# Inverse transform of a spectral-filter and feed-forward kernel: first step split over two sums of 64 frequencies, last step over 16 classes, both as pairs of 64-row matmuls

## The chip, the cores and the metric

The kernel runs on one core of a Trainium2 chip. The metric is device time in microseconds of one execution, taken as the median over runs. One profiled execution of the kernel before was recorded too; all durations of single instructions come from it.

TensorE (PE) multiplies; VectorE (DVE) and ScalarE (ACT) do elementwise work and empty the matmul results out of PSUM; GpSimd (POOL) and SyncE (SP) mainly issue DMAs here. Each engine works through its own instruction list in the order in which the program wrote it.

## The reference

The input x has 2048 rows (s) and 1024 columns (d). It is normalised by row to xn. One branch is a two-dimensional real Fourier filter, the other a feed-forward layer; the result is x + filter * silu(feed-forward).

```python
xn = _layernorm(x, axis=-1)
X = rfft2(xn, axes=(-2, -1)) * (w_r + 1j * w_i)      # w: 2048 x 513
s = irfft2(X, (2048, 1024), axes=(-2, -1))
h = silu(einsum("bsd,df->bsf", xn, w1))              # w1: 1024 x 3584
g = silu(einsum("bsf,fd->bsd", h, w2))               # w2: 3584 x 1024
return x + s * g
```

## The kernel before

Numbers are kept as two fp16 halves, so that each product of fp32 quality is three matmuls (high by high, high by low, low by high). Two stages of feed-forward matmuls form the backbone of TensorE's list. The first (`mm1`, L420, tile `pa`) makes the hidden layer in 112 groups of 24 matmuls of 512 columns. The second (`mm2`, L498 to L500, tile `pb`) runs seven products of a Strassen-like scheme, each in eight blocks; a block is two halves of 21 matmuls of 512 columns, and the 56 blocks make 112 halves.

The Fourier work is woven between these matmuls. Transforms are cut into a matmul over part of the index and a small butterfly on VectorE. In order: the forward transform over d (`fd_gen`, tiles `fa`, `V`, `R`), the forward transform over s with the product by the filter (`f_gen`, 16 tiles `u`: matmuls `fx` at L902 to L904, the complex product at L972 to L986, first inverse radix-4 butterflies into `Z`, and `zq`, the two fp16 halves of the result, which goes to DRAM as `zd`), a small correction for the edge frequencies (`edge_gen`), and the inverse (`i_gen`, four chunks `c`).

A chunk of the inverse loads `zt` (2 MB of `zd`) and its matrix `kk`. It has two parts. In the first, `mat(g)` (L1110 to L1118, tile `iu`) makes 24 matmuls of 256 columns, each a sum over 128 frequencies of s; `post(g)` (L1120 to L1130) copies half of the PSUM tile with ScalarE, forms sums and differences on VectorE and a radix-4 butterfly; `split(g)` (L1132 to L1137) makes the two fp16 halves `us`. In the second, `mat2(p)` (L1141 to L1147, tile `id`) makes 24 matmuls of 256 columns over d, in 8 classes of frequencies with 128 rows, and `bfly(p)` (L1149 on) combines the classes and hands the finished 128 rows to the output. Each of `mat` and `mat2` fills a PSUM tile of two banks; there are two such tiles (`pt`), so a `mat` waits until the one two before it has been emptied.

The order of all this is written out by a planner while the program is built. `meter` (L179) adds the planned cost of each instruction to a clock for TensorE and one for VectorE, by `COST` (L177): a fixed part and a part for each element. `work()` (L1274) is called after each of the 112 groups of `mm1` and after each half of a block of `mm2`. It lets the weight loaders move, and then takes up to three steps from the background list `bg`, which holds the Fourier generators in order. A step is what a generator does up to its next `yield`; a `yield PAUSE` ends the call:

```python
clock["dve"] = max(clock["dve"], clock["pe"] - 1.0)
for _ in range(3):
    if clock["dve"] > clock["pe"] + LEAD or hold[0] or slot(bg) == PAUSE:
        break
```

with `LEAD` 1.0. A tile of `f_gen` is four steps. A chunk of `i_gen` is six steps for `mat`, `post` and `split`, a load of the next chunk, a PAUSE, and five steps for `mat2` and `bfly`; each chunk but the first begins with four PAUSEs. Between `f_gen` and the first chunk stand the steps of the edge and eight PAUSEs, in which `zt` is loaded. The 128 rows that `bfly` finishes are stored to DRAM (`sd`) and read back (`fs`) when the product that completes the same rows of the other branch is through: products 4 and 5 for chunks 1 and 3, product 6 for chunk 0 in its first four blocks and for chunk 2, the last of the order, in its last four. What is left on `bg` when the 56 blocks are through is written out behind them (L1417).

Queues: SP issues the loads of weights, of `vq`, `wq`, `zt`, `kk`, `cis`, and the output; POOL issues the stores `hd`, `zd` and some weight loads; the loads of `ht` and `kq` are issued from ScalarE's list, in order with its activations.

Of the kernel before, what the change touches and what calls it, by code (L numbers as in the profile page):

```python
# [43 lines left out]
def make_constants():  # L44
# [17 lines left out]
    kc = np.stack(_halves(k, 2.0**14), 3)

    ci = np.zeros((128, 4, 2, 256))
    idx = np.arange(64)[:, None]
    dd = np.arange(128)[None, :]
    alt = np.where(dd[0] % 2 == 0, 1.0, -1.0)
    for g in range(4):
        for h, cl in enumerate((0, 4) if g == 0 else (g, 8 - g)):
            kd = 8 * idx + cl  # L70
            ph = 2 * np.pi * ((kd * dd) % 1024) / 1024
            co, si = 2 * np.cos(ph), 2 * np.sin(ph)
            r = slice(64 * h, 64 * h + 64)
            sg = 1 if h == 0 else -1
            if g == 0:
                ci[r, g, 0] = np.concatenate([co, sg * co], 1)
                ci[r, g, 1] = np.concatenate([-si, -sg * si], 1)
            else:
                ci[r, g, 0] = np.concatenate([co, sg * si], 1)
                ci[r, g, 1] = np.concatenate([-si, sg * co], 1)  # L80
# [16 lines left out]
def spectral_ffn(ctx, tc, x, w_r, w_i, w1, w2, ca, kc, ci, tw, pm, out):  # L97
    nc = tc.nc
# [773 lines left out]
    def f_gen():  # L872
        bp = B["p"]

        def load_k(q):
# [48 lines left out]

        def high_z(u):
            q, j = u // 4, u % 4
            if j == 0:
# [1 line left out]
            nc.scalar.activation(zqs[q][:, 0, :, 16 * j:16 * j + 16], zs_[u], AF.Copy, scale=zs)
# [522 lines left out]
```

## Time and profile before

| | us |
|---|---|
| runs, median (lowest to highest) | 1291.36 (1288.75 to 1295.92) |
| profiled execution, span from first to last instruction | 1291.9 |
| TensorE busy in the span | 1264.8 (98%) |
| VectorE busy | 958.6 (74%) |
| ScalarE busy | 463.9 (36%) |
| GpSimd busy | 242.3 (19%) |
| DMA moved | 298.84 MB, mean 231 GB/s |
| TensorE busy with `iu` and `id`, 384 matmuls each | 45.3 and 43.2 |

The profile gives no time of its execution other than the span. Busy time is a union: matmuls overlap, so a group's busy time is less than count times mean. The `mm1` stage lies from about 23 to 645 us, the `mm2` stage from 645 us to the end, `f_gen` from about 585 to 885 us and the inverse from 945 to 1202 us.

### The profile page before, as it was taken

What the parts mean: (1) busy time and instruction counts of PE and PEld (TensorE: products, weight loads), DVE (VectorE), ACT (ScalarE), POOL (GpSimd) and SP (SyncE); (2) the same over time, 40 slices, a digit from 0 to 9 for tenths busy, and PEclk for the clock granted to TensorE, in tenths of its full rate; (3) what the DMA queues carried; (4) which work ended last, traced back from release to release, by engine and by line L of the source; (5) the groups of instructions that cost most, each with busy time, mean ns of one, the idle gap of its engine ahead of it and who ended that gap; (6) DMA issues with size and microseconds to landing.
All of it is one profiled execution on the core that took longest, in us unless ns stands there. A gap on an engine that the chain in (4) does not pass through costs nothing.

```text
span 1291.9 us, 18825 instructions
## 1 busy us (share of the span) xinstructions
PE 1264.8 (98%) x6991; PEld 656.7 (51%) x6991; DVE 958.6 (74%) x1964; ACT 463.9 (36%) x572; POOL 242.3 (19%) x389
## 2 busy tenths in 40 slices
PE   8999999999999999999999999999979999999997
PEld 5544445444544454445455555554445555656444
DVE  6688898899879898867679798993165565867544
ACT  4864343343545565534242311220131321333111
POOL 1231222223233443241221010104110100000000
PEclk9998999999999999999999999999989999999999
DMA  7576476555766896579889999984996799675995
GB/s 232 132 188 178 123 227 191 164 149 181 230 194 236 278 296 205 190 230 269 179 252 259 270 278 199 336 213 146 305 259 229 218 323 339 241 285 167 313 360 187
DMA packets 174955, 298.84 MB, mean 231 GB/s; under 512 B 38928, under 2 KB 91920, under 8 KB 174224
## 3 DMA queue, kind: packets, MB, share of 16 engines
q1 hardware_dynamic: 132464, 163.34, 42.5%
q0 software_dynamic: 26560, 82.86, 21.3%
q10 hardware_dynamic: 15840, 51.45, 11.3%
q8 instruction: 55, 0.90, 0.3%
q14 instruction: 36, 0.29, 0.1%
HBM read 189.06 MB, written 104.33 MB: 227 GB/s over the span
## 4 chain that ended last, share of the span: by engine, by line
PE 82%; DMA 8%; DVE 5%; ACT 2%; issue 2%; POOL 1%; SPq 0%; ACTq 0%; DVEq 0%; POOLq 0%
PE pa L420 39%; PE pb L498 10%; PE pb L499 10%; PE pb L500 10%; PE iu L1117 3%; PE id L1146 3%; DMA jr<-ws 2%; DMA hd_one<-hoone 2%; PE fx L902 1%; DMA zt<-zd 1%; ACT xp L657 1%; DMA jr<-in_B_w_dram 1%; DVE w L219 1%; DMA ht<-hd_sum 1%; PE fx L904 1%
## 5 line engine op out<-in xcount | busy, mean ns | idle before, releaser
L420 PE MATMUL pa<-xnT,w 128*128 128x512 f16 x2688 | 587.7, 380 | 5.6 <-DMA xnT<-xs 3.2
L420 PEld LDWEIGHTS <-w 128*128 128x128 f16 x2688 | 263.2, 98 | 319.0 <-issue 8.3
L498 PE MATMUL pb<-w,ht 128*128 128x512 f16 (+1 forms) x798 | 299.5, 375 | 0.2 <-DMA ht<-hd_sum_d 0.2
L499 PE MATMUL pb<-w,ht 128*128 128x512 f16 (+1 forms) x798 | 299.5, 375 | 0.0
L500 PE MATMUL pb<-w,ht 128*128 128x512 f16 (+1 forms) x798 | 299.5, 375 | 0.0
L429 ACT ACTIVATE h<-pa,s 128x512 f32<-128x512 f32 x112 | 75.8, 680 | 142.5 <-PE pa L420 135.7
L500 PEld LDWEIGHTS <-ht 128*128 128x128 f16 x798 | 78.1, 98 | 91.1
L498 PEld LDWEIGHTS <-ht 128*128 128x128 f16 x798 | 78.2, 98 | 88.5 <-DMA ht<-hd_sum_d 0.7
L499 PEld LDWEIGHTS <-ht 128*128 128x128 f16 x798 | 78.1, 98 | 87.8
L216 ACT ACTIVATE w<-jr,sc 128x512 f16<-128x512 f32 x98 | 67.7, 713 | 85.3 <-DMA jr<-in_B_w_dram 39.8
L219 DVE SCALAR_TENSOR_TENSOR w<-jr,sc,w 128x512 f16<-128x512 f32 x98 | 72.1, 748 | 25.9 <-ACT w L216 25.8
L219 DVE SCALAR_TENSOR_TENSOR hoone<-h,hs,hoone 128x2048 f16<-128x2048 f32 x28 | 65.8, 2348 | 19.6 <-ACT hoone L216 19.6
L452 POOL DMA_DIRECT2D hd_sum<-hosum x52 | 38.0, 767 | 209.8 <-DVE hosum L219 101.7
L216 ACT ACTIVATE hoone<-h,hs 128x2048 f16<-128x2048 f32 x28 | 55.9, 1997 | 40.3 <-DMA hd_one<-hoone 27.9
L216 ACT ACTIVATE hosum<-hr,hs 128x1536 f16<-128x1536 f32 x28 | 44.1, 1574 | 59.4 <-DVE hr L459 32.1
L452 POOL DMA_DIRECT2D hd_one<-hoone x52 | 45.5, 875 | 86.5 <-DVE hoone L219 52.5
L380 POOL DMA_DIRECT2D jr<-in_B_w_dram x28 | 24.6, 966 | 165.0 <-DMA jr<-in_B_w_dram 129.6
L458 DVE TENSOR_TENSOR hr<-h 128x1024 f32<-128x1024 f32 x28 | 34.2, 1223 | 28.0 <-ACT h L429 27.8
L1117 PE MATMUL iu<-kk,zt 128*128 128x256 f16 x384 | 45.3, 280 | 8.7 <-issue 8.7
L219 DVE SCALAR_TENSOR_TENSOR hosum<-hr,hs,hosum 128x1536 f16<-128x1536 f32 x28 | 50.8, 1814 | 1.9 <-ACT hosum L216 1.9
L216 ACT ACTIVATE w<-w1r,rs 128x1024 f16<-128x1024 f32 x28 | 32.0, 1146 | 49.6 <-DVE rs L247 20.2
L579 ACT ACTIVATE pl<-pl,c 128x512 f32<-128x512 f32 (+1 forms) x26 | 16.9, 682 | 89.5 <-DVE pl L558 45.9
(195 smaller groups left out, 1686.0 us busy)
## 6 DMA issues: line engine op xcount, KB each, us to landing
w1r<-in_B_w_dram SPq DMA_DIRECT2D x28, 512.0 KB, 6.2
w2m<-in_B_w_dram SPq DMA_DIRECT2D x28, 512.0 KB, 5.0
ht<-hd_dif ACTq DMA_DIRECT2D x32, 448.0 KB, 7.9
jr<-in_B_w_dram SPq DMA_DIRECT2D x56, 256.0 KB, 7.3
ht<-hd_sum ACTq DMA_DIRECT2D x32, 448.0 KB, 6.2
ht<-hd_one ACTq DMA_DIRECT2D x32, 448.0 KB, 5.2
hd_sum<-hosum POOLq DMA_DIRECT2D x52, 256.0 KB, 3.4
hd_one<-hoone POOLq DMA_DIRECT2D x52, 256.0 KB, 5.1
```

The source lines that it names most:

```text
L216: nc.scalar.activation(hi, raw, AF.Copy, scale=scale)
L219: nc.vector.scalar_tensor_tensor(lo, raw, scale, hi, op0=OP.mult, op1=OP.subtract)
L380: nc.gpsimd.dma_start(raw[n], w2_block(*todo[n], 1), accum_op=OP.add)
L420: nc.tensor.matmul(ps, w[:, wh, d], xt[:, xh, d], start=(n == 0), stop=(n == 23))
L429: nc.scalar.activation(hq[:, 2 * (c % 2) + f % 2], ps, AF.Silu, scale=s1[:, f:f + 1])
L452: defer(1, lambda k=k, m=m: stores[0].dma_start(hd[m, g][:, :, q].rearrange("f p h s -> f p (h s)"), o[:, k].rearrange("f p h s -> f p (h ...
L458: tt(sums[:, 0:2], hq[:, 0::2], hq[:, 1::2], op=OP.subtract)
L498: nc.tensor.matmul(ps, hh[:, 0], w[:, 0], start=first, stop=False)
L499: nc.tensor.matmul(ps, hh[:, 0], w[:, 1], start=False, stop=False)
L500: nc.tensor.matmul(ps, hh[:, 1], w[:, 0], start=False, stop=last)
L1117: nc.tensor.matmul(ps[:, q], lhs, rhs, start=(n == 0 and r == 0), stop=(n == 2 and r == 1))
L1146: nc.tensor.matmul(o, us[g][:, uh, 2 * p + r], C["ci"][:, ch, g, r], start=(n == 0 and r == 0), stop=(n == 2 and r == 1))
```

## The change

Both inverse steps are recast so that a sum runs over 64 rows and not 128. Two such sums, one on partitions 0 to 63 and one on 64 to 127, are issued one after the other and write to the two banks of the PSUM tile. The frequencies of s are reordered in the constants (`m1_of`), so that the even ones lie in the lower 64 partitions, and `kk` has half its columns; the filter weights are loaded in two DMAs of 64 partitions each to have the same order. Frequencies of d are stored in 16 classes of 32 and no longer 8 of 64. Instructions of `mat` and `mat2` double in number, with 128 columns and not 256. VectorE then has to combine the two sums: `post` and `bfly` get new sums, differences and rotations. In `f_gen` the reordering moves from the butterfly (twelve small operations become one `radix4` of four) to the making of the halves (one activation and one VectorE operation become six each); the scale `zs` is applied to the filter weights by two activations per tile. The planner gets other constants, and a matmul over 64 partitions is counted at half its price.

```diff
-    COST = {"DVE": ("dve", 0.12, 1.05e-3), "PE": ("pe", 0.0, 0.4215e-3)}
+    COST = {"DVE": ("dve", 0.07, 1.045e-3), "PE": ("pe", 0.0025, 0.4167e-3)}
...
-            clock[name] += fixed + each * max(rows)
+            halves = 2 if name == "pe" and inst.ins[0].ap[0][1] == 64 else 1
+            clock[name] += (fixed + each * max(rows)) / halves
...
-                nc.sync.dma_start(t_, wv[i][q][:, :, 128 * j:128 * j + 128])
+                for b in range(2):
+                    nc.sync.dma_start(t_[64 * b:64 * b + 64], wv[i][q][b, :, :, 128 * j:128 * j + 128])
...
+        def by_class(u):
+            j = u % 4
+            zv = zs_[u].rearrange("m n (i h l) -> m n h l i", h=2, l=8)
+            qv = [zqs[u // 4][:, k].rearrange("m (n g b) i -> m n b g i", g=4, b=4)[:, :, :, :, 8 * j:8 * j + 8] for k in range(2)]
+            first = [v[:, :, :, 0].rearrange("m n (l h) i -> m n h l i", h=2) for v in qv]
+            for z, o in ((zv[:, :, :, 1:4], [v[:, :, 0:4:3, 3:0:-1] for v in qv]),
+                         (zv[:, :, :, 5:8], [v[:, :, 2:0:-1, 1:4] for v in qv]),
+                         (zv[:, :, :, 0:8:4], first)):
+                yield z, o
...
-            nc.scalar.activation(zqs[q][:, 0, :, 16 * j:16 * j + 16], zs_[u], AF.Copy, scale=zs)
+            for z, o in by_class(u):
+                for h in range(2):
+                    nc.scalar.activation(o[0][:, :, h], z[:, :, h], AF.Copy)
...
-            nc.vector.scalar_tensor_tensor(zq[:, 1, :, zsl], zs_.pop(u), zs, zq[:, 0, :, zsl], op0=OP.mult, op1=OP.subtract)
+            for z, o in by_class(u):
+                for h in range(2):
+                    nc.vector.tensor_tensor(o[1][:, :, h], z[:, :, h], o[0][:, :, h], op=OP.subtract)
...
+            for w in (wr, wi):
+                nc.scalar.activation(w, w, AF.Copy, scale=zs)
...
-            Z = bp.tile([128, 8, 8, 16], F32, name=f"Z{u}", tag="X", bufs=2)
...
+            Z = bp.tile([128, 8, 128], F32, name=f"Z{u}", tag="X", bufs=2)
+            radix4(1, b2, d2, Z)
...
-            ps = pt.tile([128, 4, 256], F32, name=f"iu{c}_{g}", tag="ft")
+            ps = pt.tile([128, 2, 4, 128], F32, name=f"iu{c}_{g}", tag="ft")
...
-                        nc.tensor.matmul(ps[:, q], lhs, rhs, start=(n == 0 and r == 0), stop=(n == 2 and r == 1))
+                        for b in range(2):
+                            rows_ = slice(64 * b, 64 * b + 64)
+                            lhs = zt[rows_, q, zh, r, 4 * g:4 * g + 4].rearrange("m l i -> m (l i)")
+                            rhs = k[rows_, q, kh, 1 - r:3 - r].rearrange("m r a -> m (r a)")
+                            nc.tensor.matmul(ps[:, b, q], lhs, rhs, start=(n == 0 and r == 0), stop=(n == 2 and r == 1))
...
-            tt(b.rearrange("m c r k -> m c (r k)"), ps[:, 0:2], cpy, op=OP.add)
-            tt(d.rearrange("m c r k -> m c (r k)"), ps[:, 0:2], cpy, op=OP.subtract)
+            tt(w[:, 0], ps[:, 0], cpy, op=OP.add)
+            tt(w[:, 1], ps[:, 0], cpy, op=OP.subtract)
+            sums, dif, turn = w[:, 0], w[:, 1], w[:, 2]
+            nc.vector.tensor_single_scalar(dif[:, 1:4:2], dif[:, 1:4:2], RH, op=OP.mult)
+            tt(turn[:, 0:4:3, 0], dif[:, 1:4:2, 0], dif[:, 1:4:2, 1], op=OP.subtract)
+            tt(turn[:, 1:3, 0], dif[:, 1:4:2, 0], dif[:, 1:4:2, 1], op=OP.add)
+            bv, dv = (v.rearrange("m c r (e a) -> m e c r a", e=2) for v in (b, d))
+            tt(bv[:, 0], sums[:, 0:2], sums[:, 2:4], op=OP.add)
+            tt(dv[:, 0], sums[:, 0:2], sums[:, 2:4], op=OP.subtract)
+            for j, x_, y_ in ((0, dif[:, 0], dif[:, 2, ::-1]), (1, turn[:, 0:2, 0], turn[:, 2:4, 0])):
+                tt(bv[:, 1, j, 0], x_[:, 0], y_[:, 0], op=OP.subtract)
...
-                        nc.tensor.matmul(o, us[g][:, uh, 2 * p + r], C["ci"][:, ch, g, r], start=(n == 0 and r == 0), stop=(n == 2 and r == 1))
+                        for half in range(2):
+                            rows_ = slice(64 * half, 64 * half + 64)
+                            nc.tensor.matmul(ps[:, half, g], us[g][rows_, uh, 2 * p + r], C["ci"][rows_, ch, g, r], start=(n == 0 and r == 0), stop=(n == 2 and r == 1))
...
-            tt(pqf[:, 0], ps[:, 0, 0], cpy[:, 0], op=OP.add)
...
+            tt(w[:, 0], ps[:, 0], cpy, op=OP.add)
+            tt(w[:, 1], ps[:, 0], cpy, op=OP.subtract)
+            t_ = ip.tile([128, 3, 2, 64], F32, name=f"st{c}_{p}", tag="so", bufs=1)
+            nc.vector.tensor_single_scalar(t_[:, 0:3:2], w[:, 1, 1:4:2], C16, op=OP.mult)
+            nc.vector.tensor_single_scalar(t_[:, 1], w[:, 1, 2], RH, op=OP.mult)
+            d3, d1, o3, o2, o1 = w[:, 1, 1], w[:, 1, 3], w[:, 2, 1], w[:, 2, 2], w[:, 2, 3]
+            stt(o1[:, 0], d1[:, 1], -S16, t_[:, 2, 0], op0=OP.mult, op1=OP.add)
...
+            tt(pqv[:, 0], w[:, 0:2, 0], y2, op=OP.add)
...
```

Left out above: the twelve strided operations that made `Z`; in `post` three more operations of 64 elements for each of the two `j`; in `bfly` the other five operations of 64 elements and three more of 256 like the last one shown. What follows them in `post` and `bfly` stays.

More of the change, by code (lines that the diff above doesn't have):

```diff
@@ L60, in make_constants @@
     th = 2 * np.pi * (((4 * a + c) * (4 * m1 + q)) % 2048) / 2048
+    row = np.arange(128)
+    m1_of = 2 * (row % 64) + row // 64
     k = np.stack([-np.sin(th), np.cos(th), np.sin(th)], 3)
[L62 to L66, printed above, removed]
+    kf = np.stack(_halves(k[..., m1_of], 2.0**14), 3)
+    ki = np.stack(_halves(k[:, m1_of, :, :, :64], 2.0**14), 3)
+    kc = np.concatenate([kf.reshape(4, 128, -1), ki.reshape(4, 128, -1)], 2)
+    ci = np.zeros((128, 4, 2, 2, 64))
+    idx = np.arange(32)[:, None]
+    dd = np.arange(64)[None, :]
     alt = np.where(dd[0] % 2 == 0, 1.0, -1.0)
     for g in range(4):
[L69 to L80, printed above, removed]
+        for half, first in enumerate((-g % 4, 4 + g)):
+            for e, cl in enumerate((0, 8) if first == 0 else (first, 16 - first)):
+                kd = 16 * idx + cl
+                ph = 2 * np.pi * ((kd * dd) % 1024) / 1024
+                co, si = 2 * np.cos(ph), 2 * np.sin(ph)
+                r = slice(64 * half + 32 * e, 64 * half + 32 * e + 32)
+                sg = 1 if e == 0 else -1
+                if first == 0:
+                    ci[r, g, 0] = np.stack([co, sg * co], 1)
+                    ci[r, g, 1] = np.stack([-si, -sg * si], 1)
+                else:
+                    im = -1 if half else 1
+                    ci[r, g, 0] = np.stack([co, im * sg * si], 1)
+                    ci[r, g, 1] = np.stack([-si, im * sg * co], 1)
     ci[0, 0, 0] = 1.0
-    ci[0, 0, 1] = np.concatenate([alt, alt])
-    ci = np.stack(_halves(ci, 2.0**13), 1)
+    ci[0, 0, 1] = alt
+    ci = np.stack(_halves(ci.reshape(128, 4, 2, 128), 2.0**13), 1)
     j = np.arange(8)
@@ L1087, in open_i @@
         C["p"] = C["es"].enter_context(tc.tile_pool(name="inv", bufs=1, side="right"))
-        C["ci"] = C["p"].tile([128, 2, 4, 2, 256], F16, name="cis")
+        C["ci"] = C["p"].tile([128, 2, 4, 2, 128], F16, name="cis")
         C["z"], C["k"] = {}, {}
@@ L1118, in mat @@
             psu[g] = ps
         def post(g):
[L1121 to L1123 removed]
+            ps = psu.pop(g).rearrange("m b q (r a) -> m b q r a", r=2)
+            w = ip.tile([128, 3, 4, 2, 64], F32, name=f"uw{c}_{g}", tag="uc", bufs=1)
+            cpy = w[:, 2]
+            nc.scalar.activation(cpy, ps[:, 1], AF.Copy)
             b = ip.tile([128, 2, 2, 128], F32, name=f"ub{c}_{g}", tag="ub", bufs=1)
@@ L1147, in mat2 @@
             psd[p] = ps
         def bfly(p):
-            ps = psd.pop(p)
-            cpy = ip.tile([128, 2, 256], F32, name=f"sc{c}_{p}", tag="uc", bufs=1)
-            nc.scalar.activation(cpy, ps[:, :, 1], AF.Copy)
+            ps = psd.pop(p).rearrange("s h g (r d) -> s h g r d", r=2)
+            w = ip.tile([128, 3, 4, 2, 64], F32, name=f"sw{c}_{p}", tag="uc", bufs=1)
+            cpy = w[:, 2]
+            nc.scalar.activation(cpy, ps[:, 1], AF.Copy)
+            tt(w[:, 0], ps[:, 0], cpy, op=OP.add)
```

62 lines of the change are left out of this document (31 added, 31 removed).

## The prediction

> **What bounds the kernel now.** I read the page's totals first, then its chain of waits, then busy time by stretches.
>
> ```profile
> span 1291.9 us, 18825 instructions
> PE 1264.8 (98%) x6991; PEld 656.7 (51%) x6991; DVE 958.6 (74%) x1964; ACT 463.9 (36%) x572; POOL 242.3 (19%) x389
> ...
> PE 82%; DMA 8%; DVE 5%; ACT 2%; issue 2%; POOL 1%; SPq 0%; ACTq 0%; DVEq 0%; POOLq 0%
> ```
>
> TensorE has work in all but 27 us, and is 82% of the chain. What takes TensorE time away shortens the end, as long as nothing makes it wait.
>
> The stretches (columns: stretch, its length, PE, PEld, DVE, ACT, POOL busy with counts, granted clock, DMA share, GB/s) are four filter tiles, the start of the inverse, the inverse, and what is behind it:
>
> ```profile
> 723.00:788.00 65.00, 65.00 (x398) 34.73 (x397) 60.66 (x133) 17.34 (x25) 3.48 (x5) 1.00 0.95 264
> 900.00:945.00 45.00, 36.63 (x170) 16.46 (x168) 11.37 (x18) 10.11 (x16) 11.72 (x14) 0.94 0.99 289
> 945.00:1199.00 254.00, 253.65 (x1546) 152.29 (x1547) 166.68 (x405) 67.46 (x101) 11.34 (x14) 0.99 0.77 257
> 1199.00:1292.00 93.00, 86.34 (x443) 43.01 (x440) 43.48 (x82) 15.00 (x24) 0.00 (x0) 0.98 0.82 286
> ```
>
> TensorE is full in the filter and the inverse, but in the filter VectorE (93%) and the DMA engines (0.95) are close behind. TensorE idles 8.4 us ahead of the inverse and 6.7 us at the end.
>
> **The matmuls, the gain.** The fine order on TensorE shows the price of a matmul as the distance between starts:
>
> ```profile
> 757.36 0.27 PE L902 MATMUL fx<-vq,kq 128*128 128x256 f16 x1
> 757.47 0.22 PE L903 MATMUL fx<-vq,kq 128*128 128x128 f16 x1
> 757.53 0.22 PE L904 MATMUL fx<-vq,kq 128*128 128x128 f16 x1
> 757.58 0.27 PE L902 MATMUL fx<-vq,kq 128*128 128x256 f16 x1
> ...
> 959.37 0.38 PE L499 MATMUL pb<-w,ht 128*128 128x512 f16 x1
> 959.59 0.38 PE L500 MATMUL pb<-w,ht 128*128 128x512 f16 x1
> 959.80 2.78 PE L1117 MATMUL iu<-kk,zt 128*128 128x256 f16 x24
> 962.42 0.38 PE L498 MATMUL pb<-w,ht 128*128 128x512 f16 x1
> ```
>
> 24 inverse matmuls of 256 columns take 962.42 - 959.80 = 2.62 us, 0.109 each; one of 128 columns takes 0.055, its own weight load included (757.47 to 757.58 for two). `iu` and `id` are 768 matmuls, 83.8 us. The change makes 768 pairs of 128 columns. No row shows two 64-row matmuls side by side, so a pair lies between 0.055 (fully together) and 0.111 (one after the other). Loads overlap already: L903's last 0.098 by their mean, and start every 0.055:
>
> ```profile
> L903 PEld LDWEIGHTS <-kq 128*128 128x128 f16 x192 | 18.8, 98 | 1.5
> ```
>
> So I take a pair near the lower end, 0.060: 768 x (0.109 - 0.060) = **-37.6 us**; the ends are -41.5 and +1.4.
>
> A change between full and half array may empty the pipeline: a 512-column matmul is on record for 0.38 us where the next starts after 0.216, so up to 0.16 us each time. With about six groups of `mat` per chunk there are 48 changes: 0 to 7.9 us, I take **+4**, the middle. The Trainium skill, "TensorEngine Tiling (Array Packing)", section "Tiling Modes", says that changing the mode drains the engine. By it this term would be 7.9 and the sum 3.9 later.
>
> **VectorE, the price.** Its row spacing, contiguous and strided:
>
> ```profile
> 764.92 0.39 DVE L997 TENSOR_TENSOR Z<-yb 128x128 f32<-128x128 f32 x1
> 765.22 0.39 DVE L998 TENSOR_TENSOR Z<-yd 128x128 f32<-128x128 f32 x1
> ...
> 766.79 0.21 DVE L996 TENSOR_TENSOR Z<-yb 128x32 f32<-128x32 f32 x1
> 766.92 0.20 DVE L997 TENSOR_TENSOR Z<-yb 128x32 f32<-128x32 f32 x1
> ...
> 767.29 0.74 DVE L219 SCALAR_TENSOR_TENSOR w<-jr,sc,w 128x512 f16<-128x512 f32 x1
> ...
> 769.21 0.68 DVE L953 TENSOR_TENSOR xb<-fx,xc 128x512 f32<-128x512 f32 x1
> 769.81 0.68 DVE L954 TENSOR_TENSOR xd<-fx,xc 128x512 f32<-128x512 f32 x1
> 770.41 0.42 DVE L203 TENSOR_TENSOR X<-xb 128x256 f32<-128x256 f32 x1
> 770.74 0.42 DVE L204 TENSOR_TENSOR X<-xb 128x256 f32<-128x256 f32 x1
> ...
> 776.56 1.28 DVE L934 SCALAR_TENSOR_TENSOR zq<-Z,zs,zq 128x1024 f16<-128x1024 f32 x1 [4.06 <-ACT zq L929]
> 777.76 1.22 DVE L972 TENSOR_TENSOR T<-X,wq 128x1024 f32<-128x1024 f32 x1
> 778.90 1.22 DVE L973 TENSOR_TENSOR T<-X,wq 128x1024 f32<-128x1024 f32 x1
> ...
> 981.39 0.29 DVE L1167 TENSOR_TENSOR s<-spq,sab 128x128 f32<-128x128 f32 x1
> 981.60 0.28 DVE L1168 TENSOR_TENSOR s<-spq,sab 128x128 f32<-128x128 f32 x1
> ```
>
> Contiguous: 0.60 for 512 elements, 0.335 for 256, 0.205 for 128, so 0.14 for 64 on the same line. Strided as in `Z`: 0.30 for 128, 0.13 for 32, about 1.77 ns an element and 0.07.
>
> `post` takes 2 x 0.60 + 4 x 0.335 = 2.5 now; after it 2 x 0.60 + 0.335 + 2 x 0.205 + 2 x 0.335 + 8 x 0.14 + 4 x 0.335 = 5.1. `bfly` takes 4 x 0.335 + 10 x 0.20 = 3.4 now; after it 2 x 0.60 + 0.335 + 0.205 + 6 x 0.14 + 4 x 0.335 + 2.0 = 5.9. That is 5.1 us for each of 16, **82 us more VectorE** (96 if a 64-element operation costs what one of 128 does), 20 of it in each chunk. By itself this is off the path, covered by `mm2`: without that cover it is the end.
>
> Per filter tile, `Z` costs 767.29 - 764.62 = 2.67 now and 4 x 0.335 = 1.34 after. The low half costs 1.20 (776.56 to 777.76) now, six operations after: 1.5 contiguous, 2.2 strided (`by_class` reads `Z` in steps of 16 elements, so I take 2.2). VectorE gains 0.3 of about 11. ScalarE gets five more activations and two of 512: at least 2 x 0.59 us a tile (the 512-element copy below), up to 3; it is a quarter busy, so its load is no bound, its order can be.
>
> **The planner, which decides where this lands.** The cost of an operation falls from 0.12 + 1.05 n to 0.07 + 1.045 n (n in thousands of elements); the new line is the spacing just read, the old one 0.05 above it. A half of a block gives TensorE 21 x 0.216 = 4.53 us. A filter tile was 11.6 on the planner's VectorE clock, 14 with weight halves and sums beside it: more than two halves and its matmuls give (2 x 4.53 + 2.65 = 11.7), so it took three (16.2). The stretch 723 to 788, 65 us long, confirms it by 48 matmuls of L902, 12 a tile:
>
> ```profile
> 723.00:788.00 65.00, 10.81 (x48) 4.70 (x48) 1.00 0.95 264
> ```
>
> With the new prices the tile is 10.1, 11.8 with the rest: two halves. So 14 tiles save 14 halves, and the first inverse matmul, now behind 56 of the 112 halves (392 matmuls of L498 ahead of it, seven a half), comes behind about 42:
>
> ```profile
> 640.00:945.00 305.00, 148.57 (x392) 38.43 (x392) 0.99 0.89 255
> ```
>
> ```profile
> 1013.86 7.86 PE iu L1117 x72
> ...
> 1089.21 7.86 PE iu L1117 x72
> ...
> 1155.49 7.86 PE iu L1117 x72
> ```
>
> A chunk takes 75.3 and 66.3 us in the chain's order, which is 12 and 10 halves with 192 x 0.109 of its own matmuls; five of these halves are its PAUSEs. New, its steps are 4 x (5.1 + 1.1 + 5.9) = 48.6 us of VectorE; with about 1.4 us of sums and weight halves in each half, one step now fills a call where three fitted, and I count 18 halves. Four chunks end 42 + 3 x 18 + 13 = 109 halves in, of 112. Now 19 halves are left free (443 matmuls behind 1199 us). So the cover just suffices, and this is what the change lives on.
>
> **What follows, in TensorE time.** In the filter VectorE really needs about 10.8 + 2.2 = 13.0 a tile against 11.7, and two transfers lose lead: the store of `zq` is issued just ahead of the activation that reuses it, and `wq` is loaded two halves ahead and not four, now in front of ScalarE's list (the scaling by `zs`), behind which `ht` loads and evacuations queue.
>
> ```profile
> ACT zq L929 <- DMA zd<-zq: 13.0, 2, 7.6
> PE iu L1117 <- issue: 8.7, 1, 8.7
> ...
> L923 ACT ACTIVATE xc<-fx 128x512 f32<-128x512 f32 x16 | 9.4, 590 | 30.6 <-issue 15.1 <-PE fx L904 11.1 <-DMA wq<-in_A_w_i_dram 4.4
> ```
>
> 14 x 1.3 = 18 us, and three waits of up to 7.6 + 4.5, less some 15 us of slack that the two PSUM tiles give: 0 to 25, I take **+8**. Ahead of the inverse `kk` and `cis` are halved (0.9 MB, 3 us at 289 GB/s) and the loads move off the weight loads of product 4: of the 8.7 us wait I take **-4** (-8.7 to +5). VectorE's waits inside the inverse: **+2** (0 to 8). The end, with the last chunk 3 halves from it: **+4** (0 to 25). The planner's lost margin in `mm1`, where VectorE was 85 to 90% busy, and the 48 more DMA issues on SP I cost at nothing: SP is ahead by whole tiles there; without that the `wq` wait above grows.
>
> Sum: 1291.9 - 37.6 + 4 + 8 - 4 + 2 + 4 = **1268 us**. The span is 0.5 us over the median of the runs, 1291.36, so the sum stands for the runs as it is.
>
> **Rivals.** *All hidden.* Pairs at 0.055, no wait in the filter, the wait before the inverse gone: 1291.9 - 41.5 - 8.7 + 4 = 1246. For it: VectorE's waits do not reach TensorE now, which is busy 65.00 of 65.00 us in the filter. Against: VectorE had 7% to spare there, and that goes.
>
> *Halves do not overlap.* A pair costs 0.111 because its two weight loads follow each other at 0.055: the gain becomes +1.4, the planner still counts half: 1291.9 + 1.4 + 4 + 8 - 4 + 2 = 1303. For it: each load is for 128 columns, as before. Against: 0.098 loads overlap today. The Trainium skill, "TensorE: Matmul & The Clock Gate", section "LDWEIGHTS (loading the stationary operand)", has a load priced by columns and not by rows, an estimate of 107 ns here: two would make a pair 0.21. The trace disagrees with that size, as 0.055 between starts shows, and not with the rule on rows.
>
> *The cover runs out* (slower). If the filter stays at three halves a tile, whether planned or because VectorE's other work is dearer than I counted, the inverse starts at half 56; three chunks of 18 fill it to 110, and the whole fourth chunk is written behind the 56 blocks: 48.6 us of VectorE bare, of which 4 stood in the sum: 1291.9 - 37.6 + 4 - 4 + 49 = 1303. It decides from about 1 us of VectorE more per half; each step left over costs 6.
>
> *The filter binds.* DMA at 0.95 and VectorE over 100% stall TensorE the full 25 us: 1285.
>
> **How the numbers follow.** Forecast 0.47, all hidden 0.17, filter binds 0.10, halves apart 0.12, cover out 0.14. About 0.5% (6.5 us: 1285 to 1298) is what a measurement can tell from no change. Faster: 0.45 + 0.17 + 0.04 = 0.66; same: 0.02 + 0.06 + 0.04 + 0.02 = 0.14; slower: the rest of the last two rivals, 0.08 + 0.12 = 0.20. The range goes from all hidden, 1246, to a little past the slow cases, 1305; the forecast's own is 1250 to 1285.
>
> **What would show it.** The 48 matmuls of a `mat` at 1.44 us by their starts: over 2.6 refutes the gain. `fx` groups 11.7 to 13 us apart and not 16.2; the first `iu` some 14 halves earlier in `pb`; VectorE over 80% of the span; at most three halves of `pb` after the last `id`. A bare run of `id` after the last `pb`, or TensorE waits of over 25 us in the filter, would make the prediction wrong.

## The result and the profile after

The changed kernel takes 1284.78 us (median of 4 runs, 1282.11 to 1285.19), the kernel before on the same chip 1291.89 (4 runs; the 1291.36 of the table further up is the median of three of them): a ratio of 0.9939 with a 95% interval of 0.9915 to 0.9963, so it is 0.6% faster, a little past what can be told from no change. The forecast was 1268, 1.8% faster. The profiled execution has a span of 1282.9 us against 1291.9.

The totals of the page after:

```profile
span 1282.9 us, 20862 instructions
...
PE 1234.2 (96%) x7759; PEld 624.8 (49%) x7759; DVE 1033.5 (81%) x2284; ACT 501.5 (39%) x684; POOL 243.0 (19%) x389
```

TensorE has 30.6 us less work and yet the span is only 9.0 us shorter: its idle time grew from 27 to 49 us. Where it idles is told by the busy time in stretches, columns as in the prediction:

```profile
660.00:723.00 63.00, 53.39 (x336) 28.90 (x333) 51.79 (x101) 26.72 (x54) 6.44 (x9) 0.94 0.75 231
723.00:788.00 65.00, 64.63 (x405) 36.56 (x406) 59.59 (x119) 28.44 (x58) 3.17 (x5) 0.95 0.80 199
788.00:853.00 65.00, 55.96 (x318) 29.84 (x317) 57.69 (x115) 22.75 (x48) 3.47 (x5) 0.92 0.76 244
900.00:945.00 45.00, 45.00 (x457) 24.09 (x456) 33.55 (x102) 9.32 (x13) 1.71 (x2) 1.00 0.55 166
1250.00:1283.00 33.00, 20.60 (x137) 13.21 (x135) 24.12 (x56) 5.93 (x10) 0.00 (x0) 0.88 0.81 286
```

Before, the filter was full (65.00 of 65.00 at clock 1.00) and TensorE idled ahead of the inverse. Now the inverse begins without a pause, and the filter has the holes: 9.6 and 9.0 us in the first and third row, each with a clock below 1. The waits of TensorE by what ended them (us in total, times, longest) name them; `eps` is the matmul of the edge correction:

```profile
PE fx L914 <- DMA vq<-vd: 9.0, 1, 9.0
PE fx L914 <- DMA jr<-ws: 6.8, 1, 6.8
...
PE iu L1141 <- DVE zt L1129: 3.5, 1, 3.5
PE pb L509 <- DMA ht<-hd_sum_d: 3.2, 1, 3.2
...
PE eps L1051 <- POOL edge L1044: 1.6, 1, 1.6
```

The 6.8 us are put down to a `jr` load (raw weights of the second stage), which `fx` does not read; it was issued between the two `vq` loads shown further down. That `fx` waited for one of these is a reading, not a row.

To compare kernels I use three quantities. In the filter (first `pb` to first `iu`) and in the inverse (first `iu` to the last matmul), *lost* is the length of the stretch less what its matmuls need at their steady spacing: 4.53 us a half (half of an `mm2` block, 21 matmuls), 2.65 a group of `fx`, 2.0 for the edge, and for the inverse matmuls the price shown next. The *tail* is what follows the last matmul.

| | before | after | difference |
|---|---|---|---|
| inverse matmuls | 83.8 | 47.7 | -36.1 |
| filter, lost (before with the 8.7 us ahead of `iu`) | 10.4 | 30.1 | +19.7 |
| inverse, lost | 2.3 | 4.6 | +2.3 |
| tail | 6.5 | 12.3 | +5.8 |
| `mm1`: end at 644.7 and 646.7, the latter with one `fx` group (2.65) more in it | | | -0.6 |
| sum (span: -9.0) | | | -8.9 |

The order on TensorE gives the price of the new matmuls:

```profile
918.70 0.38 PE L511 MATMUL pb<-w,ht 128*128 128x512 f16 x1
919.01 1.51 PE L1141 MATMUL iu<-kk,zt 64*128 64x128 f16 x48
920.45 0.39 PE L509 MATMUL pb<-w,ht 128*128 128x512 f16 x1
```

48 of them take 1.44 us, where 24 of twice the columns took 2.62. Inside, starts lie 3.5 and 52.5 ns apart in turn: 0.056 us a pair. Of the 1.44, 0.10 is the return to the full array, and the `pb` matmul ahead takes 919.01 - 918.70 = 0.31 and not 0.216. So a group pays 0.19 for its two changes; 24 groups stand between `pb` matmuls, eight of them two `mat` or `mat2` long: 768 x 0.056 + 24 x 0.19 = 47.6 us (47.7 in the table, from unrounded spacings).

What the holes cost beyond their length shows in the stretch of `fx` behind the 6.8 us wait (723.37 to 728.40; PE alone is of use here):

```profile
723.37:728.40 5.03, 5.03 (x36) 4.29 (x37) 5.03 (x13) 2.19 (x6) 0.00 (x0) 0.50 0.78 172
```

The 36 matmuls of one group run at a granted clock of 0.50, 5.03 us instead of 2.65, and the group behind the 9.0 us wait does the same (0.50 in 798.5 to 803.6 us); for 4.6 and 2.4 us behind the two groups it is 0.91 and 0.84. Behind the two short holes the clock is down too: 0.77 in 706 to 712 us, 0.86 in 856.4 to 860 and 0.80 in 860 to 866. The four waits of the filter above sum to 20.6; of the 30.1 lost 9.5 remain, where before it was 10.4 - 8.7 = 1.7. Length times the missing share of the clock, summed over the stretches behind the four holes, gives an estimate of 8.9 us, so the low clock accounts for nearly all of that rest.

One reason why the loads came late is on SP's list (waits of the queues in 640 to 860 us, after; then the same for before):

```profile
SPq L387 <- DVE w L230: 61.0, 12, 12.7
```

```profile
SPq L376 <- DVE w L219: 68.0, 17, 16.1
```

A weight load `jr` waits until VectorE has used its buffer, up to 12.7 us in the row above, and SP's list, worked through in order, has the `vq` loads behind it:

```profile
700.91 8.23 SPq L387 DMA_DIRECT2D jr<-ws  x3
...
713.60 0.55 SPq L387 DMA_DIRECT2D jr<-ws  x1
714.25 0.38 SPq L894 DMA_DIRECT2D vq<-vd  x1
714.71 0.63 SPq L387 DMA_DIRECT2D jr<-ws  x1
715.89 0.50 SPq L894 DMA_DIRECT2D vq<-vd  x1
```

The kernel before waited there just as long; with 16.4 us a tile it did not matter. After, a tile is planned at two or three halves, 12.9 us of TensorE on average (2.27 x 4.53 + 2.65), and really takes 15.4. VectorE is busy 13.25 of these and idle 2.1, and most of that waits for ScalarE, while ScalarE waits for VectorE (waits of VectorE, then of ScalarE, in 640 to 860 us):

```profile
DVE T L1002 <- ACT wq L997: 14.0, 6, 7.0
```

```profile
ACT zq L954 <- DVE Z L217: 55.7, 11, 7.0
```

So in the filter no engine is full: VectorE, ScalarE (the scaling of `wq`, the six activations for `zq`) and SP's list wait for each other in a ring, and TensorE is last in it. The DMA engines are not what is full: their share is 0.75 to 0.80 in the three rows of the filter, where it was 0.95 before.

### The profile page after: what moved, and what is told of

Its sections match the earlier page's. It is cut to its first block, busy times and chain, and to the rows that moved or that the text cites. A ratio compares the mean times of both kernels' runs of the same rounds, so it can differ in the third digit from the quotient of the medians.

```text
span 1282.9 us, 20862 instructions
## 1 busy us (share of the span) xinstructions
PE 1234.2 (96%) x7759; PEld 624.8 (49%) x7759; DVE 1033.5 (81%) x2284; ACT 501.5 (39%) x684; POOL 243.0 (19%) x389
## 3 DMA queue, kind: packets, MB, share of 16 engines
q10 hardware_dynamic: 15840, 51.45, 11.6%
## 5 line engine op out<-in xcount | busy, mean ns | idle before, releaser
L509 PE MATMUL pb<-w,ht 128*128 128x512 f16 (+1 forms) x798 | 301.6, 378 | 3.2 <-DMA ht<-hd_sum_d 3.2
L509 PEld LDWEIGHTS <-ht 128*128 128x128 f16 x798 | 78.4, 98 | 93.9 <-DMA ht<-hd_sum_d 3.4
L230 DVE SCALAR_TENSOR_TENSOR w<-jr,sc,w 128x512 f16<-128x512 f32 x98 | 71.6, 745 | 18.2 <-ACT w L227 18.2
L230 DVE SCALAR_TENSOR_TENSOR hoone<-h,hs,hoone 128x2048 f16<-128x2048 f32 x28 | 65.6, 2343 | 12.6 <-ACT hoone L227 12.6
L954 ACT ACTIVATE zq<-Z 128x192 f16<-128x192 f32 (+1 forms) x96 | 38.7, 483 | 79.3 <-DVE Z L217 58.9
L914 PE MATMUL fx<-vq,kq 128*128 128x256 f16 x192 | 47.8, 291 | 15.8 <-DMA vq<-vd 9.0
```

What stands on the lines that cost most here:

```text
L230: nc.vector.scalar_tensor_tensor(lo, raw, scale, hi, op0=OP.mult, op1=OP.subtract)
L509: nc.tensor.matmul(ps, hh[:, 0], w[:, 0], start=first, stop=False)
L914: nc.tensor.matmul(o, k[:, c, kh, 1], v[:, c, vh], start=(n == 0), stop=False)
L954: nc.scalar.activation(o[0][:, :, h], z[:, :, h], AF.Copy)
```

## The experiments

The kernel changed is the one after, except in e3. Lost, tail and span are of the profiled execution of each; "tile" is the mean distance of `fx` groups 5 to 16, "halves" are halves of `mm2` blocks. All in us; the ratio is against the kernel before on the same chip. Medians of runs on different chips are compared by these ratios.

| run | halves before `iu` | tile | filter lost | inverse lost | tail | span | median | ratio (95%) |
|---|---|---|---|---|---|---|---|---|
| before | 56 | 16.4 | 10.4 | 2.3 | 6.5 | 1291.9 | 1291.89 | |
| after | 43 | 15.4 | 30.1 | 4.6 | 12.3 | 1282.9 | 1284.78 | 0.9939 (0.9915 to 0.9963) |
| e14, after again | 43 | 14.8 | 26.2 | 5.4 | 12.0 | 1279.4 | 1283.63 | 0.9909 (0.9880 to 0.9939) |
| e1 | 43 | 15.3 | 30.8 | 11.9 | 11.9 | 1291.6 | 1293.41 | one run |
| e5 | 43 | 15.0 | 27.9 | 43.2 | 6.3 | 1314.3 | 1316.19 | one run |
| e3 | 45 | 15.3 | 30.4 | 6.2 | 6.3 | 1315.2 | 1317.08 | 1.0189 (1.0158 to 1.0220) |
| e4 | 54 | 16.2 | 1.3 | 34.9 | 19.4 | 1293.6 | 1291.53 | 0.9990 (0.9967 to 1.0013) |
| e13 | 43 | 14.6 | 18.2 | 5.1 | 12.4 | 1272.8 | 1269.94 | 0.9811 (0.9779 to 0.9842) |
| e2 | 43 | 14.6 | 33.8 | 2.5 | 12.9 | 1285.0 | 1290.40 | 0.9978 (0.9957 to 0.9999) |
| e9 | 43 | 14.1 | 23.5 | 14.2 | 11.6 | 1284.7 | 1289.54 | 0.9984 (0.9963 to 1.0006) |
| e10 | 43 | 14.2 | 25.8 | 23.1 | 6.3 | 1291.3 | 1290.84 | 0.9974 (0.9951 to 0.9997) |
| e17 | 43 | 14.8 | 32.6 | 6.9 | 11.8 | 1287.1 | 1284.84 | 0.9923 (0.9895 to 0.9952) |
| e7 | 43 | 15.1 | 27.3 | 6.0 | 6.3 | 1275.8 | 1279.97 | 0.9894 (0.9839 to 0.9950) |
| e15, e7 again | 43 | 15.3 | 31.4 | 5.2 | 6.3 | 1279.5 | 1282.37 | 0.9896 (0.9864 to 0.9928) |
| e6 | 49 | 15.9 | 14.2 | 14.3 | 14.4 | 1279.5 | 1279.30 | 0.9873 (0.9837 to 0.9909) |
| e8 | 49 | 15.6 | 11.2 | 10.8 | 15.3 | 1273.6 | 1278.15 | 0.9866 (0.9826 to 0.9906) |
| e16, e8 again | 49 | 15.3 | 7.5 | 13.4 | 14.2 | 1270.7 | 1277.67 | 0.9862 (0.9834 to 0.9890) |
| e11 | 47 | 15.9 | 22.1 | 20.0 | 8.7 | 1286.7 | 1287.06 | 0.9959 (0.9942 to 0.9977) |
| e12 | 47 | 14.4 | 13.7 | 23.0 | 9.4 | 1283.4 | 1287.02 | 0.9961 (0.9946 to 0.9975) |
| e18 | 49 | 14.7 | 0.6 | 11.0 | 15.5 | 1265.3 | 1269.41 | 0.9814 (0.9784 to 0.9844) |

The e7 kernel went from 27.3 to 31.4 us of filter loss between its two runs, and the kernel after from 30.1 to 26.2: differences of 4 us in the lost columns say nothing.

### Are the halves what makes the matmuls cheap? (e1, e5)

e1 issues six matmuls of one half, then six of the other, in `mat` (shown) and `mat2` alike:

```diff
-                for n, (zh, kh) in enumerate(((0, 0), (0, 1), (1, 0))):
-                    for r in range(2):
-                        for b in range(2):
+                for b in range(2):
+                    for n, (zh, kh) in enumerate(((0, 0), (0, 1), (1, 0))):
+                        for r in range(2):
```

> The changed kernel, with the loop over the two row halves moved outside the six matmuls of a sum, so that matmuls of the same half follow each other and pairs no longer alternate. Theory (the gain comes from two neighbouring matmuls of different halves running together): 48 matmuls of 128 columns cost 48 x 0.055 = 2.65 us by their starts in place of the 1.45 us of the changed kernel, TensorE gets 768 x (0.111 - 0.060) = 39 us more, and the time goes from 1285 to about 1310 to 1325. Rival (a 64-row matmul is simply cheaper by itself, or the halves overlap whatever the order): 1.45 us and 1285 as before.

```profile
914.85 1.64 PE L1141 MATMUL iu<-kk,zt 64*128 64x128 f16 x48
916.42 0.39 PE L509 MATMUL pb<-w,ht 128*128 128x512 f16 x1
```

48 take 916.42 - 914.85 = 1.57 us, 9% more than 1.44. The halves overlap even when six matmuls of one stand between; that the order of issue in pairs is needed is refuted. Nor can TensorE have started all of them strictly in the order of its list: with 0.056 us between two of the same half, as e5 shows next, eight runs of six would take 8 x 5 x 0.056 = 2.24 us and more. It started matmuls of one half ahead of earlier ones of the other. The run took longer all the same: of the 7.3 us more lost in the inverse, 32 x 0.13 = 4.2 are the matmuls and 2.2 a longer wait for `zt` (5.7 against 3.5); one run doesn't tell the rest.

e5 puts both sums on the lower half, so that the upper 64 frequencies are left out and the lower ones taken twice, in `mat` (shown) and `mat2` alike:

```diff
-                            rows_ = slice(64 * b, 64 * b + 64)
+                            rows_ = slice(0, 64)
```

> The changed kernel, with both matmuls of every inverse pair reading partitions 0 to 63, so that the sums over partitions 64 to 127 are left out and those over 0 to 63 are made twice; number, size and order of the matmuls stay. Theory (a 64-row matmul of 128 columns takes its 0.055 us like one of 128 rows, and the gain is that the two halves overlap): the 48 matmuls of a mat cost 2.6 to 2.7 us by their starts, not 1.44, and the time goes up by up to 38 us, to 1310 to 1330. Rival (a 64-row matmul is cheaper by itself, as the order in runs of six, 1.57 us, might suggest): 1.4 to 1.6 us, 1285 to 1295.

```profile
914.46 2.85 PE L1141 MATMUL iu<-kk,zt 64*128 64x128 f16 x48
917.24 0.39 PE L509 MATMUL pb<-w,ht 128*128 128x512 f16 x1
```

2.78 us for 48, 0.056 each after the 0.09 to 0.10 of the change. So a 64-row matmul alone costs what one of 128 rows costs, and the whole gain is that the other half runs beside it. In the table the 1.34 us of each of 32 groups make 42.9; the inverse lost 38.6 more, and the tail got shorter by 6 though the order is the same. So the four PAUSEs alone do not make the tail; that the dearer matmuls gave VectorE the time to catch up is a reading, which no row here shows.

### Is it the pace or the new work? (e3, e4, e13)

e3 is the kernel before with nothing changed but the planner's prices:

```diff
-    COST = {"DVE": ("dve", 0.12, 1.05e-3), "PE": ("pe", 0.0, 0.4215e-3)}
+    COST = {"DVE": ("dve", 0.07, 1.045e-3), "PE": ("pe", 0.0025, 0.4167e-3)}
```

> The kernel before, with only the planner's VectorE and TensorE constants of the change (the halving counts nothing, since no matmul spans 64 rows). Theory (the new constants alone press the filter together, and its waits come from the pace): fx groups come 11.7 to 16 us apart, TensorE loses 5 to 25 us in the filter, the wait of 8.7 us ahead of the inverse shrinks, and the time is 1290 to 1305. Rival (the waits come from the new work in each tile, the scaling on ScalarE and the doubled loads on SP): no waits in the filter, 1280 to 1292.

```profile
PE fx L902 <- DMA vq<-vd: 12.5, 3, 6.2
PE eps L1029 <- POOL edge L1022: 8.5, 1, 8.5
...
PE iu L1117 <- ACT pl L579: 4.1, 1, 4.1
```

It is 25 us slower, more than either side expected, and its filter loses 30.4, as after, with 12.5 us of waits for `vq` and 8.5 at the edge. The old matmuls and the old VectorE work do this too. Against e3, all the rest of the change is worth 1317.1 - 1284.8 = 32 us.

e4 holds every filter tile back to three halves, and takes three of the four PAUSEs of a chunk away, so that the last chunk still fits:

```diff
-            yield 2.9
+            yield PAUSE if True else 2.9
...
-            for _ in range(4):
-                yield PAUSE
+            yield PAUSE
```

> The changed kernel, with a PAUSE at the end of every filter tile, which holds it to three halves as before, and one PAUSE and not four ahead of each inverse chunk, without which the inverse would not fit. Theory (pace): the 19 us of waits in the filter and about 7 us of slow clock behind them go; the inverse starts at half 56 or so and ends in the last blocks, which costs 3 to 10 us at the end, and the wait ahead of the inverse may come back with up to 8.7: 1262 to 1278. Rival (new work in each tile): the waits stay, 1283 to 1300.

Its filter, and then its waits in the inverse (1030 to 1115 us, all engines):

```profile
723.00:788.00 65.00, 65.00 (x398) 34.73 (x396) 59.47 (x113) 27.35 (x54) 3.47 (x5) 1.00 0.86 248
```

```profile
ACT pl L590 <- DVE pl L557: 40.6, 6, 10.9
...
DVE fs L583 <- DMA fs<-gd: 10.7, 1, 10.7
PE id L1184 <- DVE sw L1193: 10.4, 1, 10.4
...
PE iu L1140 <- DVE zt L1128: 9.8, 1, 9.8
```

At the pace of before the filter loses next to nothing (1.3 us), new work or not. But the time is that of before: 34.9 us are lost in the inverse and 19.4 behind it. With the inverse 11 halves later, ScalarE and VectorE wait for the finishing of rows (`pl`, and `fs` read back from `gd`), and TensorE idles for the `id` and `iu` that stand behind them. The loss has moved, it is not gone; so the theory was right on the filter and wrong on the time.

e13 leaves the low half of `zq` out (its place is zeroed) and charges the planner for it as before, so that the order stays:

```diff
+                nc.gpsimd.memset(zqs[q][:, 1], 0.0)
...
-            for z, o in by_class(u):
-                for h in range(2):
-                    nc.vector.tensor_tensor(o[1][:, :, h], z[:, :, h], o[0][:, :, h], op=OP.subtract)
+            clock["dve"] += 4 * (0.07 + 1.045e-3 * 192) + 2 * (0.07 + 1.045e-3 * 128)
```

> The changed kernel, with the six VectorE operations that make the low half of the filter result left out (2.2 us a tile); GpSimd sets that half to zero once for four tiles, so the filter result keeps its high half only. The planner's clock is moved as if they were there, so plan and pace stay. Theory (VectorE sets the filter tile): the tile falls from 15.4 to 13.0 to 13.6 us, the filter loses 8 to 15 us and not 30, and the time is 1263 to 1275. Rival (the order of loads sets it): tile over 14.8 us, loss over 24, 1280 to 1290.

Its waits of VectorE in 640 to 880 us:

```profile
DVE T L1001 <- ACT wq L996: 34.6, 13, 10.3
```

Beside e14 on the same chip it is 13.7 us faster by the medians (6.6 by the two spans, and 8.0 in the filter's loss). So VectorE's 2.2 us a tile are a part of the loss. In their place VectorE now waits for the scaled `wq`, 34.6 us where it was 14.0; a tile still takes 14.6 with 10.8 us of VectorE work in it, and `fx` still waits 13.4 us for `vq`. The time came out in the theory's range, the tile and the loss between the two. So VectorE's time is one cause and not the whole; that the rest is late loads is tested by e18 further down.

### Can a queue be relieved alone? (e2, e9, e10, e17)

e2 issues the `vq` load on GpSimd, not behind the weight loads on SP:

```diff
-                nc.sync.dma_start(t_, vd[j][:, q])
+                nc.gpsimd.dma_start(t_, vd[j][:, q])
```

> The changed kernel, with the 16 loads of vq issued from GpSimd's queue and not from SP's. Theory (the two waits of fx, 6.8 and 9.0 us with slow-clock matmuls behind them, come from vq loads standing in SP's list behind weight loads that wait for VectorE): both waits go, some 16 + 5 us, and the time is 1262 to 1272. Rival (VectorE and the DMA engines are simply too slow for the pace of the filter): the waits stay or move to other places, 1280 to 1290.

```profile
PE eps L1051 <- POOL edge L1044: 9.1, 1, 9.1
PE fx L914 <- DMA vq<-vd: 7.7, 2, 6.5
PE fx L914 <- ACT zq L954: 4.5, 1, 4.5
```

The waits of the filter sum to 23.9 with 2.6 of a `pb` matmul for `ht`, where it was 20.6. The edge now waits for GpSimd, and `fx` for ScalarE; `vq` still comes late. So the place of `vq` behind the weight loads is not the cause by itself.

e9 loads weights three blocks ahead and not four, so that fewer `jr` stand before `vq`; e10 adds to it one PAUSE a chunk and the store of `zq` without its delay:

```diff
-        for n in range(4):
+        for n in range(3):
...
-            load(n + 4)
+            load(n + 3)
```

> The changed kernel, with the loads of the second weights (jr) issued three and not four pieces ahead, on the same six buffers, so that SP waits less often for VectorE to free one. Theory (vq and wq stand behind jr loads on SP's list, and that sets the 15.4 us that a filter tile really takes): SP's 61 us of waits for VectorE fall to less than half, the filter loses 10 to 15 us less, and the time is 1265 to 1278. Rival (the filter tile is bound by VectorE, ScalarE and the store of zq): the tile stays at 15 us or more and the time within 5 us of 1285.

> The changed kernel with three edits together: one PAUSE ahead of each inverse chunk, the stores of zq at once, the jr loads three ahead. Theory: if the SP order sets the filter tile, the filter loses under 15 us and the end 6: 1258 to 1270. Rival (as with one PAUSE alone): 1275 to 1283.

A tile falls to 14.1 and the filter's loss a little, but SP's waits for VectorE in 640 to 860 us only from 61.0 to 49.0 and not by half, and `fx` still waits 9.1 us for `vq`; so the theory of SP's order was hardly put to the test. The inverse loses 9 us more in e9, where `iu` waits 9.8 us for the copy of `zt` (the small VectorE operation that puts the edge's values into `zt`; 3.5 after), and 18 more in e10, where three such waits make 12.1 and one for VectorE's `uw` 3.6. No gain, and e10's time is outside both of its ranges.

e17 is e13 with the `wq` loads on GpSimd:

```diff
-                    nc.sync.dma_start(t_[64 * b:64 * b + 64], wv[i][q][b, :, :, 128 * j:128 * j + 128])
+                    nc.gpsimd.dma_start(t_[64 * b:64 * b + 64], wv[i][q][b, :, :, 128 * j:128 * j + 128])
```

> The kernel with the low half of the filter result left out, with the 64 loads of wq issued from GpSimd's queue and not SP's. Theory (the second cause is that wq stands behind weight loads on SP's list): VectorE's 34.6 us of waits for the scaling fall under 15, the filter loses under 12 us and not 18, and the time is 1258 to 1267. Rival (wq is late by the transfer itself or by its place in the program): the waits stay over 25 us, 1268 to 1280.

```profile
POOL xsv L985 <- DVE X L217: 60.9, 3, 28.5
POOL zq L952 <- DMA zd<-zq: 34.8, 3, 15.7
```

It decides nothing. On GpSimd a copy into `xsv` waits for VectorE and the zeroing that stands in for the low half waits for the store of `zq`, and the `wq` loads queue behind both: the experiment made a new queue of its own.

### What does the end cost? (e7, e15)

One PAUSE at the start of a chunk in place of four, and nothing else:

```diff
-            for _ in range(4):
-                yield PAUSE
+            yield PAUSE
```

> The changed kernel, with one PAUSE ahead of each inverse chunk in place of four, and nothing else. Theory: the filter loses its 19 us of waits and 7 us of slow clock as before; the inverse ends some 9 halves earlier, so that the 12.4 us behind the last matmul shrink to about 7, against up to 10 us of waits for zt, whose lead falls: 1278 to 1290. Rival (the end is not set by the late inverse): the 12.4 us stay.

> The changed kernel with one PAUSE ahead of each inverse chunk, again. Theory (the late end costs 6 us): 5 us less than the changed kernel on the same chip, 1278 to 1283. Rival (the earlier difference was the chip): within 2 us of it.

The last chunk ends with 399 `pb` matmuls to come and not 210 (17 halves and not 8, as the last 84 matmuls have half the columns), and the tail is 6.3, as before the change. In time this is worth little: 1282.4 against 1283.6 on the same chip, with intervals that overlap.

### Between two and three halves (e6, e8, e11, e12, e14, e16, e18)

If the filter wants time and the inverse wants an early start, a tile of two halves and one of three in turn should beat both. e6 holds every second tile, with one PAUSE a chunk; e8 and e16 also store `zq` without the delay, ahead of the activation that reuses it:

```diff
-                    defer(1, lambda c=c: stores[0].dma_start(zd[c][:, q], zv[:, :, c]))
+                    stores[0].dma_start(zd[c][:, q], zv[:, :, c])
...
-            yield 2.9
+            yield PAUSE if u % 2 else 2.9
```

> The changed kernel, with a PAUSE at the end of every second filter tile (about 2.5 halves a tile) and one PAUSE ahead of each inverse chunk in place of four. Theory (the loss moves between filter and inverse with the pace, and each side forgives a few us of lag before TensorE stops): the first iu comes 48 to 50 halves behind the start of mm2, the waits in the filter fall from 19 us to under 6, chunk 1 is ready for product 4 and nothing is stored and read back, TensorE idles under 15 us in the inverse and at the end: 1262 to 1275. Rival (the work behind mm2 is bound by VectorE and its chain whatever the pace): 1282 to 1295.

> As the run with every second filter tile held, and the four stores of a finished zq issued at once and not a half later. Theory (the activation that reuses zq waits for the store, and loads of ht behind it on ScalarE's list come late): ScalarE's wait for the store falls by about 4.5 us in each of three places, and the time by 0 to 5 us against the run without it. Rival (that wait is covered at this pace): no difference over 2 us.

> The changed kernel itself, on the chip of the two variants beside it. Both theories: 1283 to 1288, ratio 0.992 to 0.996.

> The changed kernel with every second filter tile held, one PAUSE ahead of each chunk and the stores of zq at once, again. Theory (lag shared between filter and inverse): 6 to 8 us less than the changed kernel on the same chip. Rival (the earlier difference was the chip): within 2 us of it.

The three times lie above e6's theory, 1262 to 1275. The inverse starts behind 49 halves, the filter loses about half as much or less, the inverse 5 to 10 us more and the tail 2 to 3. e16 is 6.0 us under e14 on the same chip. That the early store adds to e6 is not shown (1278.15 and 1279.30).

e11 is e8 with every third tile held, e12 that with the weight loads of e9:

```diff
-            yield PAUSE if u % 2 else 2.9
+            yield PAUSE if u % 3 == 1 else 2.9
```

> The changed kernel with one PAUSE ahead of each chunk, the stores of zq at once, and every third filter tile held by a PAUSE. Theory (the loss moves between filter and end): first iu behind 46 to 48 halves, 12 to 18 us lost in the filter, 8 to 12 us behind the last matmul, 1272 to 1280, between the runs with none and with every second tile held. Rival (there is an optimum where both are hidden): under 1270.

> As the run with every third tile held, with the jr loads three pieces ahead as well. Theory (SP order): 4 to 10 us less than that run. Rival: within 3 us of it.

```profile
ACT w L227 <- DMA jr<-in_B_w_dram: 28.3, 7, 8.7
...
PE iu L1140 <- DVE zt L1128: 16.3, 1, 16.3
```

Both lie between the kernel after and before. Both missed their theory. In e12 (1030 to 1090 us) the copy for `zt` stands on VectorE's list behind a `bfly` and the finishing of rows. That `bfly` started late by 5.8 us, as the copy that ScalarE makes for it stood behind a weight half whose load was late; then VectorE worked without a break for 12.6 us up to the copy, and TensorE waited 16.3 us for it. The hold is thus not a matter of "more is better": where it puts the inverse against the weight loads counts as much.

e18 is e8 with the `wq` loads on GpSimd, by the edit of e17; the low half is made as in e8:

> The changed kernel with every second filter tile held, one PAUSE ahead of each chunk, the stores of zq at once, and the loads of wq on GpSimd's queue. Theory (SP order as second cause): the filter loses under 5 us and not 7.5 to 11, 1270 to 1276. Rival (at this pace the order of SP is covered, and GpSimd's own waits come in): 1277 to 1290.

The filter of e18 by stretches, GpSimd's waits in it, and VectorE's waits in e16 and then in e18 (waits in 640 to 880 us):

```profile
723.00:788.00 65.00, 65.00 (x398) 34.70 (x397) 58.14 (x115) 29.72 (x60) 13.16 (x22) 1.00 0.97 252
```

```profile
POOL wq L902 <- DVE T L1002: 88.1, 8, 15.2
```

```profile
DVE zq L960 <- ACT zq L954: 16.6, 3, 6.9
```

```profile
DVE T L1002 <- ACT wq L997: 7.3, 5, 3.6
...
DVE zq L960 <- ACT zq L954: 5.9, 2, 3.3
```

The filter is full at clock 1.00 with a tile of 14.7 us, and loses 0.6, at a DMA share of 0.97, so the DMA engines do not bind at 0.75 to 0.80. The `wq` loads wait 88.1 us for their buffers, but on GpSimd, where no `vq` load stands behind them: the 5.2 us for which `fx` waited for `vq` in e16 are gone, and VectorE waits 5.9 us for ScalarE's `zq` where it waited 16.6. The time is 1269.41, a ratio of 0.9814 (0.9784 to 0.9844), the best of the versions that leave nothing out: 24 us under the kernel before on its chip and, by the ratios, 12 to 16 us under the one after. Against e16 (0.9862, on another chip) it is about 6 us, near the edge of what the two intervals allow; the loss in the filter, 0.6 against 7.5, is past the 4 us of scatter seen above. What is left in it is 11.0 lost in the inverse, of which 8.2 are two waits of `iu` for the copy of `zt`, and the tail of 15.5; an earlier place for that copy was not tried.

## Why the prediction was right and wrong

**Matmuls, right.** Pairs at 0.060 with 4 us for the changes were forecast, 33.6 us net; 36.1 were measured. A group pays 0.09 and 0.10 us for going to the half array and back, below the 0.16 that bounded each; the 24 groups forecast are the 24 counted. That it pays at all agrees with the draining of which the Trainium skill, "TensorEngine Tiling (Array Packing)", section "Tiling Modes", speaks. The rival "halves do not overlap" fell, as a pair costs 0.056 us and not 0.111. A price of 107 ns a load, an estimate from the Trainium skill, "TensorE: Matmul & The Clock Gate", section "LDWEIGHTS (loading the stationary operand)", is refuted for this use: 0.056 us covers two matmuls with a load each.

**VectorE's work, right.** `post` was forecast at 5.1 and takes 912.62 + 0.34 - 907.68 = 5.3 between these rows (5.0 without the pauses between), `bfly` at 5.9 and takes 6.1, the low half 2.2 and takes 2.18; VectorE in all +77 forecast (82 in the inverse, less 0.3 in each of 16 filter tiles), +75 measured.

```profile
703.64 2.18 DVE L960 TENSOR_TENSOR zq<-Z,zq 128x192 f16<-128x192 f32 x6
...
907.68 0.69 DVE L1151 TENSOR_TENSOR uw<-iu,uw 128x512 f32<-128x512 f32 x1 [5.80 <-ACT uw L1148]
...
912.62 0.42 DVE L217 TENSOR_TENSOR uu<-ud 128x256 f32<-128x256 f32 x1
...
940.93 0.69 DVE L1193 TENSOR_TENSOR sw<-id,sw 128x512 f32<-128x512 f32 x1 [0.77 <-ACT sw L1192]
...
946.82 0.28 DVE L1227 SCALAR_TENSOR_TENSOR s<-so,spq 128x128 f32<-128x128 f32 x1
```

**The planner's counts, right.** 43 halves ahead of the inverse (about 42 forecast); this row counts its 301 matmuls of L509, seven a half:

```profile
640.00:905.40 265.40, 115.94 (x301) 29.85 (x301) 0.95 0.79 242
```

The chunks took 16 to 18 halves (18) and ended 8 halves before the end (3), so the cover did not run out.

**The filter, wrong: this step failed.** The sum had +8 there, 0 to 25; it was about +28 (19.7, and the 8.7 us ahead of `iu` that are gone from the same stretch), and 27 of it are the eleven distances of the table's tile, 15.4 us where the plan gives TensorE 12.9. The sign named for it was TensorE waits of over 25 us in the filter; the waits are 20.6, so by the letter it did not come, but with the low clock behind them 30.1 were lost. Its own terms, 18.2 and three waits of 12.1 less 15, reach 39.5 if each wait comes in full, further than the 25 written as the bound. Three pieces of the step were off. First, 15 us were taken off for the slack of two PSUM tiles, which no row showed. A tile needs 15.4 us and not 13.0, because VectorE's 13.25 have 2.1 of waiting beside them, and slack is used up once while the pace is short on every tile. Second, 48 more issues on SP were costed at nothing since SP was taken to be ahead by whole tiles. Its own queue had 68.0 us of waits in 17 for VectorE before the change, so it was ahead only as long as the pace left room; the prediction shows no row of that queue. Third, the sum had no term for the clock: a hole of 7 or 9 us is followed by one group of `fx` at half of it, 2.4 us more each time, and all four holes by an estimated 8.9. e3 and e4 together show that the pace opens the holes. e13 shows that VectorE's time is a part of them, and e18 against e16, at a slower pace and on another chip, that the place of the `wq` loads is another. How the loss divides between the two stays open. The rival "the filter binds", with 0.10, gave 1285. It names the stage that failed, but DMA was at 0.75 to 0.80 and not the limit that it named, and that its number fits is partly luck: its 25 in the filter and its -4 ahead of the inverse were really 28.4 and -8.7.

**Ahead of the inverse.** -4 was taken; the whole 8.7 went. **Inverse waits:** +2, measured +2.3. **The end:** +4, measured +5.8. In e7 it goes with three of the four PAUSEs; but in e5, where the matmuls take longer, it goes with all four in place.

**The difference.** From the sum, 1268, to the span of 1282.9 are 14.9 us: filter +20.4, end +1.8 and inverse waits +0.3, less 4.7 ahead of the inverse, 2.5 of the matmuls and 0.6 in `mm1`, make 14.7. The median of the runs lies 1.9 above that span. This is a small error of the sum too: in every run that has both, the time is 1.7 to 2.0 us above the span, so a sum that starts from a span does not stand for the runs as it is.

## What to carry to other kernels

Before an order is tightened, look at the queues' own waits in the stretch (what is late already, and what slack hides it), not only at the busy shares of the engines: a ring of engines can bind with none of them full (here VectorE at 86% and ScalarE at 40% in the filter tiles). Change a planner's prices in a run by themselves; in the kernel before they alone cost 25 us. A filter that must slow down and an inverse that must start early are tuned against each other, one tile at a time, and in these runs moving a load from the slowest list to another queue was seen to help only together with that.

## What the runs showed of the hardware

Two streams of 64-row matmuls on the two halves overlap without being interleaved: six of one and then six of the other still give 1.57 us for 48 (e1), against 1.44 in pairs and 2.78 on one half (e5), so TensorE starts matmuls of one half ahead of earlier ones of the other. The return from half to full array costs about as much as the entry (0.10 and 0.09 us). And after idle times of 6.8 and 9.0 us TensorE ran at a clock of 0.50 for more than 5 us before it came back; with the shorter stretches behind 3.2 and 1.6 us the holes of the filter, 20.6 us in the waits, cost an estimated 8.9 us more.
